# Moving the first stage of batch 2 to later groups, in quarter tiles of the array

## The chip, the cores and the metric

One core of one Trainium2 chip runs the whole program. The metric is device time in microseconds (us) from the start to the end of one launch. The engines are TensorE (PE, its weight loads PEld), VectorE (DVE), ScalarE (ACT), GpSimd (POOL) and SyncE (SP), which issues most of the transfers.

## What is computed

The input x is eight batches of 3008 tokens of 256 float32 values. Each batch is filtered along the tokens by a Fourier transform and then goes through two matrix products with a shrink between them:

```python
X = np.fft.rfft(x, axis=1)
y = np.fft.irfft(X * (filt_r + 1j * filt_i), n=3008, axis=1)
h = y.reshape(24064, 256) @ w_in        # 256 -> 2048
out = (h - np.tanh(h)) @ w_out          # 2048 -> 256
```

## The kernel before

**Stages.** The 3008 tokens are taken as 64 x 47. The transform of a batch has three stages on TensorE. The *first stage* multiplies the 64 direction by constant matrices: r and 47 - r are the upper and lower 64 partitions of one tile, with r from 0 to 23; its result goes to a DRAM tensor `ct1[b]`. The *middle stage* (`middle`, L467 on) reads `ct1`, does the 47 direction, the filter product (four wide multiplications at L489, then L494 to L500) and the way back, and writes `ct2[b]`. The *last stage* (`last`, L565 on; its matmuls at L576) makes the tokens of one group from `ct2`.

**Groups and passes.** A batch has six groups, c = 0 to 5, of up to 512 tokens. The main loop at the end of the kernel goes through 48 groups in passes U of a quarter of the 2048 columns each, so group i has passes 4i to 4i + 3. Pass U computes the first product (`up`, its matmuls at L617 into the banks x, y and z), shrinks the pass before (`shrink`, L739 its multiplications) and computes the second product of the pass before that (`down`, L787). Batch 0's first group uses plain forms (L687 and L842). In a pass, ACT copies x (L623) and VectorE combines: L640 reads bank y, L657 bank z with the third product of x, L665 the last state of x, L673 the last state of z. Banks exist once, so the next pass's product into x waits for L665, and the product that closes z (z<-ut in the trace) waits for L657.

**The order.** It is written out by hand: every engine runs its instructions in program order. A pass has five slots, k = 0 to 4, at which `t(k)` may put one more piece of work. A position is written (c, u, k): group in its batch, pass in the group, slot. First `t` issues up to four transfers of the list `outs` on SP; then it advances one generator: the last stage for the next group at (u, k) = (3, 2), or a step of the first stage when its due position is reached, or a step at a position of `SPLIT_AT`, or the next item of `plan`, the middle stage's list. The plan has fixed kinds of slot: "there" at (2, 0), "back" at (1, 3) and "filter" at (2, 2), (2, 4), (3, 0), (3, 1), (3, 4), (0, 0), (0, 4), (1, 0) and (1, 1). If another piece takes a slot, the plan waits for the next slot of its kind.

**Weights.** They come as 64-bit words and are converted to float32 while the first groups run. VectorE does nearly all of that (L182 to L200, sums at L228 and L231): two instructions at each slot of the first passes and more between, through pass 7.

**First stage, full-array form.** `first` (L277) takes four r at a time: four matmuls of 128 x 128 weights on 256 columns (L297), two into each of the banks t and y; ACT copies both banks (L299) and issues the write of `ct1` itself (L302). Six steps make a batch. Batch 1's last four steps and batch 2's six run from one generator `fs`, due at ten positions between 4 and 31; batch 2's fall into passes 3 (two), 4, 5, 6 and 8. The one of pass 6 lies at the slot (2, 2) of group 1.

**First stage, split form.** `split_first` (L306) takes eight r at a time for batches 3 to 7, on 32 x 32 tiles. It first forms the sum and the difference of two halves on VectorE (L331 and L333, 128 x 1024 each), then runs 32 matmuls (L340) into four banks. ACT copies three banks (L345 to L347), VectorE adds and subtracts (L348, L349), and eight writes go to `outs`. Three steps make a batch; each is five calls of the generator.

A float32 matmul of the program stands as two records of PE in the trace. A timeline row joins records of one group; its start of the next row minus its own start is the time that it holds the engine.

Of the kernel before, what the change touches and what calls it, by code (L numbers as in the profile page):

```python
# [9 lines left out]
F32 = mybir.dt.float32  # L10
# [7 lines left out]
BATCH, SEQ, DM = 8, 3008, 256  # L18
NQ, NR = 64, 47
NA = NQ // 2  # L20
NH = (NR + 1) // 2
# [95 lines left out]
def kernel(  # L117
# [156 lines left out]
        turns[tag] = 1 - turns.get(tag, 1)  # L274
        return kept[tag][:, turns[tag]]

    def first(b, z, also=()):  # L277

        jobs = [*also, *((b, c) for c in range(NX))]

        def begin(k):
            b, c = jobs[k]
            f = tr.tile([128, XH, 128], F32, tag="f", bufs=2, name="f")
            w = XH * 128
            nc.sync.dma_start(f, both_d[:, w * c:w * (c + 1)])
            return load_x(tr.tile([128, XH, DM], F32, tag="x", bufs=2, name="x_sb"),
                          b, XH * c, XH), f

        began = [begin(0), begin(1)]
        yield  # L290
        for k, (b, c) in enumerate(jobs):
            xt, f = began.pop(0)
            banks = z("pf", [128, 2, DM])
            a1 = tr.tile([128, 2, 2, DM], F32, tag="a1", bufs=1, name="a1")
            for m, bank in enumerate(banks):
                for n in range(2):
                    nc.tensor.matmul(bank[:, n], f[:, 2 * m + n], xt[:, 2 * m + n],  # L297
                                     start=True, stop=True)
                ACT.copy(a1[:, m], bank)  # L299
            if k + 2 < len(jobs):  # L300
                began.append(begin(k + 2))
            ACT.dma_start(dram(ct1[b], XH * c * DM, [[NH * DM, 128], [1, XH * DM]]),  # L302
                          a1.rearrange("p m n c -> p (m n c)"))
            yield

    def split_first(b, z):  # L306

        quarters = [slice(32 * k, 32 * k + 32) for k in range(4)]
        for c, tags in enumerate((("t", "o1", "y", "o0"), ("t", "o3", "o1", "o2"),
                                  ("t", "o1", "y", "o0"))):  # L310
            f = tr.tile([128, XH, 128], F32, tag="f", bufs=2, name="f")[:, 0:2]
            f = f.rearrange("p a (b n) -> p (a b) n", n=32)
            nc.sync.dma_start(f, split_d[:, 256 * c:256 * c + 256])
            x0, x1 = (tr.tile([128, XH, DM], F32, tag="x", bufs=2, name="x_sb") for _ in range(2))
            for h, t in enumerate((x0, x1)):
                at = b * SEQ + 32 * h * NR
                for g in range(2):
                    r = 2 * FH * c + FH * g
                    low, high = quarters[g], quarters[2 + g]
                    nc.sync.dma_start(t[low], dram(x.tensor, (at + r) * DM,  # L320
                                                   [[NR * DM, 32], [1, FH * DM]]))
                    lo = int(r == 0)
                    if lo:
                        nc.sync.dma_start(t[high, 0], dram(x.tensor, at * DM,
                                                           [[NR * DM, 32], [1, DM]]))
                    nc.sync.dma_start(t[high, lo:FH], dram(x.tensor, (at + NR - r - lo) * DM,
                                                           [[NR * DM, 32], [-DM, FH - lo], [1, DM]]))
            yield
            both = tr.tile([128, 2, 2, DM], F32, tag="a1", bufs=1, name="a1")
            even = both.rearrange("p v n c -> p (v n) c")  # L330
            V.tensor_add(even, x0, x1)  # L331
            yield
            V.tensor_sub(x1, x0, x1)  # L333
# [12 lines left out]
            ACT.copy(other, banks[1])  # L346
            for g, a1 in enumerate(made):  # L347
                V.tensor_add(a1[:, 0], other if g else banks[0], a1[:, 1])  # L348
                V.tensor_sub(a1[:, 1], other if g else banks[0], a1[:, 1])  # L349
                outs[:0] = [(dram(ct1[b], ((1 - j % 2) * NH + 2 * FH * c + FH * g +  # L350
                                           2 * (j // 2)) * DM,
                                  [[2 * NH * DM, 32], [64 * NH * DM, 2], [1, 2 * DM]]),
                             a1[part].rearrange("p v n c -> p v (n c)"))
                            for j, part in enumerate(quarters)]
                yield

    SPLIT_AT = {(0, 0, 2), (0, 1, 0), (0, 1, 3), (1, 1, 1), (1, 1, 4), (2, 0, 2),
                (3, 0, 2), (4, 2, 0), (4, 2, 2), (4, 3, 0), (5, 0, 2), (5, 1, 0), (5, 1, 3),
                (5, 2, 2)}
# [629 lines left out]
    with tc.tile_pool(name="tr", bufs=2) as tr, tc.manual_schedule():  # L989
# [16 lines left out]
        with tc.tile_pool(name="pro", bufs=1) as pro, \  # L1006
# [230 lines left out]
            rest(0, SG * (last_g - 1), [nc.sync])  # L1237
            way_back()
            rest(SG * (last_g - 1), NA - SG * (last_g - 1), [nc.sync])
            fs = first(2, z2, [(1, c) for c in range(2, NX)])  # L1240
            next(fs)
            convert(100)
            late = weights(tiles1, jobs[5:], G, ahead, 3,
# [6 lines left out]
        with tc.tile_pool(name="dn", bufs=2) as dn, \  # L1250
# [60 lines left out]
                                 start=True, stop=True)  # L1311
            for _ in range(4):
                next(late)
            due = [4 + (LEAD - 4) * k / (NX + 4) for k in range(NX + 4)]
            plan = []
            kinds = {(2, 0): "there", (1, 3): "back"}
            kinds.update({at: "filter" for at in FILTERED})

            firsts, mids = {2: fs}, {}
            for U in range(total + 2):  # L1320
                i, u = divmod(U, 4)
                if U == 6:
# [4 lines left out]
                if U < total:  # L1327
# [5 lines left out]
                    if u == 2 and i + 1 < len(groups) and c + 1 == NC:  # L1333
                        assert not plan
                        e2s[i + 1] = load_e2(*groups[i + 1])
                    if u == 3 and c + 1 == NC and p + 3 < BATCH:
                        firsts[p + 3] = split_first(p + 3, zd4)
                        next(firsts[p + 3])
# [27 lines left out]
                def t(k):  # L1366
# [12 lines left out]
                    if (u, k) == (3, 2) and i + 1 < len(groups):  # L1379
                        next(last(i + 1, z2))  # L1380
                    elif due and due[0] <= pos and (U < 4 or u < 3 and k == 2):
                        due.pop(0)
                        next(firsts[2])
                    elif (c, u, k) in SPLIT_AT and 0 < p < BATCH - 2:
                        next(firsts[p + 2])
                    elif plan and plan[0] == kinds.get((u, k)):
                        plan.pop(0)
                        next(mids[p + 1])
# [58 lines left out]
```

## Time and profile before

| | us |
|---|---|
| median of 3 runs (2563.33 to 2565.52) | 2564.09 |
| the profiled execution, its time | 2566.24 |
| its span, first to last instruction | 2564.4 |
| PE busy | 2540.9 (99%) |
| DVE busy | 1878.4 (73%) |
| ACT busy | 1666.3 (65%) |
| POOL busy | 1481.4 (58%) |

All times below are from the span's start in the profiled execution. The busy share is an average over stages; what a piece of work is worth depends on which engine is full where it stands.

### The profile page before, as it was taken

The numbers are of one execution on the slowest core, as the hardware profiler recorded it, in microseconds if no ns is written. First come the engines' busy times: TensorE is split into PE (matmuls) and PEld (weight loads), VectorE is DVE, ScalarE is ACT, GpSimd is POOL, SyncE is SP. The second block draws the span as 40 slices with busy tenths as digits, with TensorE's granted clock in tenths as the row PEclk, the third lists the DMA queues.
The fourth block names the chain that finished last, engine by engine and source line by source line (L and its number), as shares of the span: only waits on it lengthen the run. The fifth ranks groups of instructions, "written<-read, shape, count | busy, mean of one in ns | idle before, by whom it ended". The sixth has DMA issues, their size and how long they took to land.

```text
span 2564.4 us, 44624 instructions
## 1 busy us (share of the span) xinstructions
PE 2540.9 (99%) x17076; PEld 2177.8 (85%) x17076; DVE 1878.4 (73%) x2265; ACT 1666.3 (65%) x2497; POOL 1481.4 (58%) x1124
## 2 busy tenths in 40 slices
PE   8999999999999999999999999999999999999998
PEld 7678888888898888988888888898889888898887
DVE  6788776887678876788668886688866877555555
ACT  4566666666666666666666666676666666666665
POOL 4256665666466655666656665566645666555552
PEclk9999999999999999999999999999999999999999
DMA  8873214422343323342233322443123322110110
GB/s 221 260 198 103 65 35 109 119 67 48 76 118 93 80 54 94 82 108 67 72 94 90 92 67 61 101 105 97 36 64 88 93 66 52 26 32 18 26 21 19
DMA packets 333660, 212.43 MB, mean 83 GB/s; under 512 B 231737, under 2 KB 304855, under 8 KB 329789
## 3 DMA queue, kind: packets, MB, share of 16 engines
q1 hardware_dynamic: 318511, 184.59, 29.5%
q0 software_dynamic: 11424, 17.03, 2.4%
q10 hardware_dynamic: 3502, 7.87, 0.9%
q8 instruction: 136, 2.23, 0.4%
q14 instruction: 87, 0.71, 0.1%
HBM read 128.75 MB, written 83.39 MB: 83 GB/s over the span
## 4 chain that ended last, share of the span: by engine, by line
PE 94%; DMA 2%; DVE 1%; ACT 1%; issue 1%; POOL 0%; ACTq 0%; POOLq 0%; DVEq 0%
PE o L787 43%; PE x L617 25%; PE z L617 12%; PE y L617 6%; PE pm L401 3%; PE pu L576 2%; DMA ct<-a 1%; PE pm L340 1%; DMA raw<-in_moe_w_in_dram 0%; DMA fh<-f 0%; DMA mats_sb<-mats 0%; PE pe L1089 0%; PE o L842 0%; PE pf L297 0%; PE warm L1038 0%
## 5 line engine op out<-in xcount | busy, mean ns | idle before, releaser
L787 PE MATMUL o<-t,wd 128*128 128x256 f32 (+1 forms) x3008 | 763.6, 377 | 0.0
L597 POOL TENSOR_TENSOR t<-h 128x512 f32<-128x512 f32 (+1 forms) x186 | 305.7, 1643 | 712.4 <-DVE h L739 703.9
L739 DVE TENSOR_TENSOR h<-h,y 128x1024 f32<-128x1024 f32 (+1 forms) x384 | 579.8, 1510 | 160.8 <-ACT y L735 157.3
L787 PEld LDWEIGHTS o<-t,wd 128*128 128x128 f32 x3008 | 569.3, 190 | 85.3 <-POOL o L815 15.1
L617 PE MATMUL x<-tu,wu 128*128 128x256 f32 (+1 forms) x2256 | 576.2, 378 | 0.2 <-ACT u L623 0.2
L787 PE MATMUL o<-h,wd 128*128 128x256 f32 (+1 forms) x2256 | 573.6, 377 | 1.8 <-DVE h L739 1.8
L787 PEld LDWEIGHTS o<-h,wd 128*128 128x128 f32 x2256 | 426.0, 190 | 72.8 <-issue 18.4
L623 ACT COPY s<-x 128x512 f32<-128x512 f32 (+1 forms) x188 | 108.6, 578 | 564.6 <-PE x L617 564.6
L617 PEld LDWEIGHTS x<-tu,wu 128*128 128x128 f32 x2256 | 423.6, 190 | 57.2 <-issue 3.7
L732 ACT ACTIVATE y<-y 128x1024 f32<-128x1024 f32 (+1 forms) x384 | 399.4, 1040 | 12.1
L735 ACT ACTIVATE y<-y 128x1024 f32<-128x1024 f32 (+1 forms) x384 | 399.8, 1041 | 4.6
L729 ACT ACTIVATE y<-h 128x1024 f32<-128x1024 f32 (+1 forms) x384 | 400.5, 1043 | 3.6 <-DVE h L665 1.7
L598 POOL TENSOR_TENSOR t<-h,t 128x512 f32<-128x512 f32 (+1 forms) x186 | 313.9, 1688 | 14.6
L600 POOL TENSOR_TENSOR t<-h,t 128x512 f32<-128x512 f32 (+1 forms) x186 | 303.7, 1633 | 0.0
L599 POOL TENSOR_TENSOR t<-h 128x512 f32<-128x512 f32 (+1 forms) x186 | 289.7, 1557 | 0.0
L623 ACT COPY u<-x 128x512 f32<-128x512 f32 (+1 forms) x376 | 213.3, 567 | 57.0 <-PE x L617 53.7
L665 DVE COPY h<-x 128x512 f32<-128x512 f32 (+1 forms) x188 | 127.8, 680 | 127.2 <-PE x L617 127.1
L617 PE MATMUL z<-tu,wu 128*128 128x256 f32 (+1 forms) x752 | 190.2, 376 | 0.4 <-DVE h L673 0.4
L617 PE MATMUL z<-ut,wu 128*128 128x256 f32 (+1 forms) x752 | 190.2, 376 | 0.4 <-DVE h L657 0.4
L617 PE MATMUL y<-ut,wu 128*128 128x256 f32 (+1 forms) x752 | 190.2, 376 | 0.0
L617 PE MATMUL x<-ut,wu 128*128 128x256 f32 (+1 forms) x752 | 190.2, 376 | 0.0
L657 DVE TENSOR_TENSOR h<-z,u 128x512 f32<-128x512 f32 (+1 forms) x188 | 127.2, 677 | 72.1 <-ACT u L623 71.1
(198 smaller groups left out, 2815.7 us busy)
## 6 DMA issues: line engine op xcount, KB each, us to landing
ft<-filt SPq DMA_DIRECT2D x28, 1024.0 KB
ct<-nn SPq DMA_DIRECT2D x56, 512.0 KB
e<-ct SPq DMA_DIRECT2D x47, 512.0 KB
a<-ct SPq DMA_DIRECT2D x112, 192.0 KB
out_dram<-ot SPq DMA_DIRECT2D x1248, 16.0 KB
x_sb<-in_x_dram SPq DMA_DIRECT2D x110, 128.0 KB
ct<-a SPq DMA_DIRECT2D x60, 128.0 KB
ct<-x_sb SPq DMA_DIRECT2D x60, 128.0 KB
```

What stands on the lines that cost most here:

```text
L597: by.tensor_sub(t[0], b[0][1], b[0][0])
L598: by.tensor_sub(t[1], b[1][1], t[0])
L599: by.tensor_sub(t[2], b[1][1], b[0][1])
L600: by.tensor_sub(t[3], b[1][0], t[1])
L617: nc.tensor.matmul(bank[:, k], wu[:, q - 1, (2 * u + k) * 128:(2 * u + k + 1) * 128], rhs[q - 1], start=(first and k == 0), stop=True, ski ...
L623: ACT.copy(t, X)
L665: V.tensor_copy(h[:, 2, :, 0:w], X)
L729: ACT.activation(y[k], ht[k], AF.Arctan, scale=TURN)
L732: ACT.activation(y[k], y[k], AF.Tanh, scale=BEND)
L735: ACT.activation(y[k], y[k], AF.Square, scale=SCALE, accum_out=y_sums[:, 2 * U + k // 2:2 * U + k // 2 + 1])
L739: V.tensor_mul(ht[k], ht[k], y[k])
L787: nc.tensor.matmul(product(q), wd[:, q - 1, (2 * u + k) * 128: (2 * u + k + 1) * 128], rhs[q - 1][:, k], start=(u == 0 and k == 0 and q == ...
```

## The change

Batch 2's first stage leaves the generator `fs`. `first` now makes steps 2 to 5 of batch 1 alone, at the same four positions as before (4, 7, 10 and 13). A new generator `second_batch` makes batch 2 at the nine positions of `SECOND_AT`, in groups 2 to 5 of batch 0. It has four steps of a new form and one split step:

- `halves_first` takes four r as before, but with weights of 64 x 64: eight matmuls on 256 columns, on the four quarters of the array, the upper and the lower partitions of the data into the two banks t and y. ACT copies bank y, VectorE adds and subtracts (two operations of 128 x 512), and two writes of `ct1` go to the head of `outs`, for SP. Its constants are half as large. It stands at (2, 0, 2), (3, 0, 2), (4, 0, 2) and (5, 0, 2); its first loads are issued at the start of pass 7, the others when a step has run.
- `split_first` with its third step alone, into the banks t, o3, o1 and o2: loads at (5, 0, 3), VectorE's sum and difference at (5, 1, 1) and (5, 1, 2), the matmuls at (5, 2, 0), the rest at (5, 2, 2).

In what follows a step of the new form is called a quarter step. The first one stands where the sixth full-array step stood, in pass 8. The slot (2, 2) of group 1 is no longer taken.

```diff
-    def first(b, z, also=()):
-        jobs = [*also, *((b, c) for c in range(NX))]
+    def first(b, z, at):
+        jobs = [(b, c) for c in at]
...
+    def halves_first(b, z, at):
+        def begin(c):
+            f = tr.tile([128, XH, 128], F32, tag="f", bufs=2, name="f")[:, :, 0:64]
+            nc.sync.dma_start(f, f_d[:, XH * 64 * c:XH * 64 * (c + 1)])
+            return load_x(tr.tile([128, XH, DM], F32, tag="x", bufs=2, name="x_sb"),
+                          b, XH * c, XH), f
+        began = [begin(c) for c in at[:2]]
+        yield
+        for c in at:
+            xt, f = began.pop(0)
+            banks = z("pf", [128, 2, DM])
+            a1 = tr.tile([128, 2, 2, DM], F32, tag="a1", bufs=1, name="a1")
+            for n in range(2):
+                for bank, half in zip(banks, rows):
+                    for m, out_half in enumerate(rows):
+                        nc.tensor.matmul(bank[out_half, n], f[half, 2 * m + n], xt[half, 2 * m + n],
+                                         start=True, stop=True)
+            if c + 2 in at:
+                began.append(begin(c + 2))
+            other = tr.tile([128, 2, DM], F32, tag="e1", bufs=2, name="other")
+            ACT.copy(other, banks[1])
+            V.tensor_add(a1[:, 0], banks[0], other)
+            V.tensor_sub(a1[:, 1], banks[0], other)
+            outs[:0] = [(dram(ct1[b], (XH * c + 2 * m) * DM,
+                              [[NH * DM, 64], [64 * NH * DM, 2], [1, 2 * DM]]),
+                         a1[part].rearrange("p v n c -> p v (n c)"))
+                        for m, part in enumerate(rows)]
+            yield
...
+    def second_batch(z, z4):
+        yield from halves_first(2, z, range(4))
+        yield from split_first(2, z4, ((2, LATE),))
+    SECOND_AT = {(2, 0, 2), (3, 0, 2), (4, 0, 2), (5, 0, 2), (5, 0, 3), (5, 1, 1), (5, 1, 2),
+                 (5, 2, 0), (5, 2, 2)}
...
-            fs = first(2, z2, [(1, c) for c in range(2, NX)])
+            fs = first(1, z2, range(2, NX))
...
-            due = [4 + (LEAD - 4) * k / (NX + 4) for k in range(NX + 4)]
+            due = [4 + (LEAD - 4) * k / (NX + 4) for k in range(4)]
...
+                    if U == 7:
+                        firsts[2] = second_batch(z2, zd4)
+                        next(firsts[2])
...
                     elif due and due[0] <= pos and (U < 4 or u < 3 and k == 2):
                         due.pop(0)
+                        next(fs)
+                    elif (c, u, k) in SECOND_AT and p == 0:
                         next(firsts[2])
```

More of the change, by code (lines that the diff above doesn't have):

```diff
@@ L304, in first, with split_first @@
             yield
-    def split_first(b, z):
+    def halves_first(b, z, at):
[26 more added lines that the diff above has]
+            yield
+    EARLY, LATE = ("t", "o1", "y", "o0"), ("t", "o3", "o1", "o2")
+    def split_first(b, z, steps=((0, EARLY), (1, LATE), (2, EARLY))):
         quarters = [slice(32 * k, 32 * k + 32) for k in range(4)]
-        for c, tags in enumerate((("t", "o1", "y", "o0"), ("t", "o3", "o1", "o2"),
-                                  ("t", "o1", "y", "o0"))):
+        for c, tags in steps:
             f = tr.tile([128, XH, 128], F32, tag="f", bufs=2, name="f")[:, 0:2]
@@ L1317 @@
             kinds.update({at: "filter" for at in FILTERED})
-            firsts, mids = {2: fs}, {}
+            firsts, mids = {}, {}
             for U in range(total + 2):
```

## The prediction

> **What bounds the kernel now.** I read the busy times by stage first, then TensorE's timeline around each step that the change touches, then VectorE's timeline there. In the rows by stage the columns are the window, its length, and the busy time of PE, PEld, DVE, ACT and POOL with instruction counts, then PE's granted clock, the DMA share and GB/s.
>
> ```profile
> core 0: us, PE busy (x) PEld busy (x) DVE busy (x) ACT busy (x) POOL busy (x), PEclk, DMA share, GB/s
> 117.30:155.00 37.70, 37.48 (x189) 24.31 (x189) 36.09 (x71) 24.80 (x42) 25.18 (x28) 1.00 1.01 281
> 155.00:170.50 15.50, 15.50 (x87) 10.49 (x86) 5.66 (x7) 9.69 (x16) 5.68 (x6) 1.00 0.86 244
> 170.50:204.70 34.20, 32.51 (x206) 27.73 (x206) 33.18 (x43) 22.97 (x34) 21.89 (x17) 1.00 0.33 86
> 220.00:429.00 209.00, 209.00 (x1436) 178.11 (x1435) 156.39 (x183) 137.92 (x205) 128.45 (x90) 1.00 0.31 76
> 373.00:380.40 7.40, 7.40 (x70) 5.79 (x69) 5.08 (x7) 5.97 (x11) 4.35 (x4) 1.00 0.00 0
> ```
>
> From 220 us on TensorE has no gap: there, every microsecond of matmul added or taken is one on the total. Before that, two stretches differ. From 117.3 to 155 VectorE is full as well (36.09 of 37.70; the rest is fractions between instructions): it converts weights. From 170.5 to 204.7 it is full again (33.18 of 34.20) and TensorE already waits (32.51). Only from 155 to 170.5 is TensorE alone the limit. So a matmul has three prices, by its place. The change takes six steps out of the early part and puts five into the part where all counts.
>
> ```profile
> 126.36 1.89 PE L297 MATMUL pf<-x_sb,f 128*128 128x256 f32 x8
> 128.09 1.67 PE L842 MATMUL o<-h,wd 128*128 128x448 f32 x4
> ...
> 152.11 1.03 PE L617 MATMUL z<-ut,wu 128*128 128x256 f32 x4
> 152.97 1.10 PE L617 MATMUL x<-ut,wu 128*128 128x256 f32 x4
> ...
> 204.81 1.89 PE L297 MATMUL pf<-x_sb,f 128*128 128x256 f32 x8
> ```
>
> A full-array step occupies TensorE from 126.36 to the next start at 128.09: 1.73 us. Batch 2 has six of them, from the row at 126.36 to that at 204.81: 10.4 us in all. If all of it counted, the change would be a gain.
>
> **Steps one to three** start between 126.36 and the row at 152.11: 5.19 us of TensorE.
>
> ```profile
> 150.47 0.68 DVE L657 TENSOR_TENSOR h<-z,u 128x512 f32<-128x512 f32 x1
> 151.07 1.21 DVE L231 TENSOR_TENSOR wd<-wd 128x256 f32<-128x256 f32 x3
> 152.20 0.68 DVE L665 COPY h<-x 128x512 f32<-128x512 f32 x1
> ```
>
> L665 reads bank x, and the next pass's first product (TensorE's row at 152.97) writes it. VectorE runs its own fixed order without a pause up to here, and none of it is work of the removed steps, so L665 still ends at 152.88. Without the three steps TensorE reaches this point 5.2 us early and waits: the start moves from 152.97 to about 152.9, a gain of **0.07 us**. Where does it wait? Product z at 152.11 needs L657, which ends at 151.15. TensorE would be ready for it at 152.11 - 5.19 = 146.9, a little later if it waits for ACT on the way. That is one idle piece of some 4 us, 0.9 us of work, and 0.8 us more of idleness.
>
> **What the idle piece does to the clock.** In the rows below, earlier in the same run, the clock column falls to 0.50.
>
> ```profile
> 53.00:56.40 3.40, 0.00 (x0) 0.00 (x0) 3.30 (x5) 0.00 (x0) 2.67 (x4) 1.00 0.94 193
> 56.40:59.80 3.40, 2.58 (x6) 2.07 (x7) 3.33 (x4) 0.58 (x1) 2.20 (x3) 0.51 0.98 306
> 59.80:63.30 3.50, 3.50 (x9) 2.61 (x9) 1.72 (x3) 0.59 (x1) 2.21 (x2) 0.50 0.58 188
> 66.70:70.10 3.40, 1.63 (x12) 1.14 (x10) 3.26 (x6) 0.85 (x2) 2.39 (x4) 1.00 0.60 159
> 70.10:73.50 3.40, 2.83 (x7) 2.09 (x7) 3.26 (x7) 0.00 (x0) 0.00 (x0) 0.51 0.83 224
> 73.50:76.90 3.40, 3.40 (x9) 2.55 (x8) 3.23 (x8) 0.58 (x1) 0.00 (x0) 0.50 0.71 246
> ```
>
> A 3.4 us stretch in which TensorE was busy for none, or for 1.63, was followed each time by some 6.8 us at half clock; the first half of each was not quite full (2.58 and 2.83 of 3.40), the second was. The 4 us piece leaves a 3.4 us stretch under half full wherever its bounds fall: the clock should drop between 148.6 (half of 3.4 after 146.9) and 152.2. It comes back after the first full stretch, between 154.0 and 159.0. What lies after 152.9 is on the path at half speed: half of 1.1 to 6.1 us, so 0.5 to 3.0; the middle of where the bounds can fall gives **+1.6 us**. [...]
>
> **Step four:**
>
> ```profile
> 159.50 1.89 PE L297 MATMUL pf<-x_sb,f 128*128 128x256 f32 x8
> ```
>
> It lies where TensorE alone is the limit and VectorE is busy 5.66 of 15.5: **-1.73 us**.
>
> **Step five** lies in the second stretch that VectorE fills; TensorE's row, then VectorE's behind it:
>
> ```profile
> 175.08 1.89 PE L297 MATMUL pf<-x_sb,f 128*128 128x256 f32 x8
> ```
>
> ```profile
> 178.75 0.69 DVE L657 TENSOR_TENSOR h<-z,u 128x512 f32<-128x512 f32 x1 [0.38 <-ACT u L623]
> 179.35 0.75 DVE L231 TENSOR_TENSOR wd<-wd 128x256 f32<-128x256 f32 x2
> 180.46 0.69 DVE L665 COPY h<-x 128x512 f32<-128x512 f32 x1 [0.36 <-PE x L617]
> 181.07 1.22 DVE L739 TENSOR_TENSOR h<-h,y 128x1024 f32<-128x1024 f32 x1
> 182.20 1.22 DVE L489 TENSOR_TENSOR nn<-xy,ft 128x1024 f32<-128x1024 f32 x1
> ```
>
> Its removal gives VectorE back its two waits behind it, 0.38 and 0.36. But the step held a slot, (2, 2) of this group, that is also a filter slot of the middle stage. Freed, it takes the filter product now at 182.20; every later one moves one slot up, and one more (1.22 us) falls into the full stretch ahead of the last wait of TensorE on it. Net **+0.48 us**; bounds: -0.74 if the extra product finds room, +1.22 if the waits stay.
>
> **Step six** (204.81) is replaced in its place by the first quarter step.
>
> **What is added.** The trace has no quarter step of 256 columns, but the last stage's product has the same tiles, 64*64 in two banks, 64 records of 64 columns: as many columns in all as the quarter step's 16 of 256.
>
> ```profile
> 244.90 0.59 PE L787 MATMUL o<-t,wd 128*128 128x256 f32 x2
> 245.43 1.16 PE L576 MATMUL pu<-gt,e 64*64 64x64 f32 x64
> 246.52 1.13 PE L617 MATMUL x<-tu,wu 128*128 128x256 f32 x4
> 247.49 1.24 PE L787 MATMUL o<-t,wd 128*128 128x256 f32 x5
> ```
>
> From 244.90 to 247.49 is 2.59 us; two 256-column records take 0.43 (an eighth of 1.73 each) and four 0.86, so the product costs 1.30 with the pauses where the tiling changes. A split step of batch 3 stands between these two rows:
>
> ```profile
> 427.66 0.92 PE L617 MATMUL x<-tu,wu 128*128 128x224 f32 x4
> ...
> 430.91 0.92 PE L617 MATMUL z<-ut,wu 128*128 128x224 f32 x4
> ```
>
> That is 3.25, less 0.75 for the four records of 224 columns and 0.86 for four of 256 that lie there too: **1.63 us** for a split step. I take **1.30 us** for a quarter step; bounds 0.86 (four records side by side, no pause) and 1.63. Step six's replacement thus gives 1.30 - 1.73 = **-0.43**, three quarter steps in groups 3 to 5 **+3.90**, the split step **+1.63**. They stand in the stretch with 209.00 busy of 209.00, and nothing covers them.
>
> **Other engines.** ACT loses twelve copies and gains seven. A quarter step gives VectorE two operations of 0.69; at its place VectorE waits for ACT's copy anyway, and I cost them at nothing (1.4 us each if that cover were gone). The split step adds two wide ones in pass 21, ahead of the copy at L665 that frees bank x for pass 22:
>
> ```profile
> L333 DVE TENSOR_TENSOR x_sb<-x_sb 128x1024 f32<-128x1024 f32 x15 | 31.6, 2106 | 0.0
> L331 DVE TENSOR_TENSOR a<-x_sb 128x1024 f32<-128x1024 f32 x15 | 23.6, 1573 | 0.0
> ```
>
> ```profile
> 380.43 0.68 DVE L665 COPY h<-x 128x512 f32<-128x512 f32 x1
> ```
>
> ```profile
> 381.90 1.03 PE L617 MATMUL x<-ut,wu 128*128 128x256 f32 x4
> ```
>
> They take 1.57 + 2.11 = 3.68; VectorE idles 7.40 - 5.79 = 1.61 of the time there, and L665 ends 0.79 before its bank is wanted, so TensorE waits 3.68 - 1.61 - 0.79 = 1.28 at most. Other cover may exist: **+1.0**, bounds 0 and 1.3. SP's queue gets fewer loads early (TensorE never waited for them); later each quarter step puts its two writes of ct1, which wait for VectorE's subtraction, at the head of the output list. Behind them wait output stores alone, and nobody reads these before the next group's transposes: no cost. In the split step eleven transfers at most stand behind VectorE's subtraction of the last quarter step; that is a rival.
>
> **The sum**: -0.07 + 1.6 - 1.73 + 0.48 - 0.43 + 3.90 + 1.63 + 1.0 = **+6.4 us**. The profiled execution took 2566.24 (span 2564.4); the median of the runs is 2564.09. Carried onto the median: **2570.5 us**, 0.25% slower. A measurement of this kernel tells about 0.2%, 5.1 us, from no change.
>
> **The rivals.**
>
> *No half clock.* The idle piece breaks up, or the clock holds: +4.8, 2568.9. For it: ACT may split the piece. Against it: both rows with under half a stretch of work were followed by 0.5. Chance 0.20.
>
> *The early steps count after all: faster.* If VectorE has 5 us of room between 117 and 155, TensorE's saving is whole: -10.4 + 4 x 1.30 + 1.63 = -3.6, 2560.5. It decides from the point where VectorE's 36.09 of 37.70 would fall below about 32. Only 1.6 us are idle, scattered. Chance 0.05.
>
> *The split step's loads are late.* They are issued after the last quarter step, and only three slots later VectorE's addition needs them. If they land 2 us late, VectorE stands, and with it L665: 2 us more, 2572.5. Against it: queue SP was idle in this stretch (DMA share 0.00 from 373.0). Chance 0.12.
>
> *The quarters do not run side by side.* Eight products one after the other take twice a full step, 3.46: four times 2.16 more, 2579.1. Against: the 64*64 row above. Chance 0.03.
>
> The forecast itself has 0.60, with 2568.5 to 2572.5 as its own range. Range for 8 in 10: 2567.0 to 2573.3. Slower by over 0.2% (above 2569.2): most of the forecast, the late loads and the serial quarters, and part of the first rival, 0.66. Within 0.2%: 0.29. Faster: 0.05.
>
> **What would show it.** PEclk at 0.5 for some microseconds near 150 to 159, and idle TensorE before it, waiting for VectorE at L657; a DVE timeline up to 155 that has not moved; the first product after it within 0.1 us of 152.9; at step five's place L489 in its stead; quarter steps 1.3 us apart; L665 late around 384. Wrong would be: VectorE's conversions ending earlier than 154, quarter steps well over 1.6 us, or TensorE gaps beyond 1.3 us in groups 2 to 5.

## The result, and the profile after

The changed kernel takes 2570.80 us (median of 9 runs, 2569.72 to 2574.22) against 2564.09 us (9 runs, 2563.33 to 2568.03). The ratio is 1.0024, with a 95% interval of 1.0015 to 1.0032: slower by 6.7 us in the medians and 6.2 by the ratio, where +6.4 was forecast. A second set gave 2571.45 us (7 runs) against 2565.09, ratio 1.0027 (1.0016 to 1.0039). The profiled execution took 2570.06 us, span 2568.3. In the changed kernel the lines named in the prediction from L489 on stand 38 lower down in the file: L617 is now L655, L657 is L695, L665 is L703, L576 is L614. The split step's addition and subtraction (L331, L333) are L363 and L365, and the quarter step's matmuls are at L323. In the experiments the numbers differ from these by a few lines.

The rows by stage of the changed kernel, columns as before:

```profile
113.00:150.80 37.80, 31.83 (x158) 18.61 (x157) 35.99 (x71) 21.47 (x36) 28.42 (x31) 0.97 0.64 170
145.00:148.40 3.40, 0.00 (x0) 0.00 (x0) 3.33 (x9) 0.00 (x0) 0.59 (x1) 1.00 0.74 177
148.50:151.91 3.41, 2.85 (x7) 2.12 (x8) 3.38 (x7) 0.00 (x0) 0.00 (x0) 0.50 1.06 255
151.90:155.30 3.40, 3.40 (x14) 2.43 (x13) 1.12 (x2) 2.75 (x4) 0.00 (x0) 1.00 0.70 211
167.20:200.00 32.80, 29.71 (x191) 24.59 (x190) 32.56 (x44) 20.33 (x30) 20.27 (x16) 1.00 0.55 134
216.00:425.00 209.00, 208.72 (x1489) 174.26 (x1488) 160.26 (x188) 136.36 (x203) 122.66 (x87) 1.00 0.39 96
```

VectorE is as full as before in the first stretch (35.99 of 37.80), and TensorE is no longer full: 31.83 busy, against 37.48. The row from 145.00 is the idle piece, the next one is at half clock. From 216 us on TensorE is full again but for 0.28 us.

TensorE's timeline of the changed kernel at the places that the forecast named:

```profile
142.53 1.67 PE L880 MATMUL o<-h,wd 128*128 128x448 f32 x4
149.06 2.07 PE L655 MATMUL z<-ut,wu 128*128 128x256 f32 x4 [4.86 <-DVE h L695]
150.93 1.53 PE L655 MATMUL x<-ut,wu 128*128 128x256 f32 x4
...
198.22 1.03 PE L655 MATMUL x<-tu,wu 128*128 128x256 f32 x4
...
201.24 0.59 PE L825 MATMUL o<-t,wd 128*128 128x256 f32 x2
201.77 1.09 PE L323 MATMUL pf<-x_sb,f 64*64 64x256 f32 x16
202.79 1.13 PE L655 MATMUL x<-tu,wu 128*128 128x256 f32 x4
...
382.43 1.13 PE L655 MATMUL x<-ut,wu 128*128 128x256 f32 x4 [0.23 <-DVE h L703]
...
2488.05 1.16 PE L614 MATMUL pu<-gt,e 64*64 64x64 f32 x64
```

The kernel before, at two places that the comparison below needs:

```profile
201.36 1.03 PE L617 MATMUL x<-tu,wu 128*128 128x256 f32 x4
...
2485.16 1.16 PE L576 MATMUL pu<-gt,e 64*64 64x64 f32 x64
```

The row at 149.06 holds the wait that the forecast described, 4.86 us for L695, and its four records take twice their time, 2.07 against 1.03. A quarter step runs from about 201.67 (two records after 201.24) to 202.79: 1.12 us, and 0.10 more in the row behind it, 1.13 against 1.03: 1.22 in all.

**How the traces are compared.** I compare by three marks, each the same record in every kernel: the product z<-ut that closes pass 4 (152.11 before, 149.06 after; called Z3), the product x<-tu 3.45 us ahead of step six (201.36 before, 198.22 after; mark 2), and the last product of the last stage (2485.16 before, 2488.05 after). Between mark 2 and the last product the change costs 6.02 us. Up to mark 2 it seems to gain 3.14 us, but the experiments show that this differs by 7 us between executions of kernels that are the same up to there. Here are the marks of all traces, and the part from mark 2 to the last product against before:

| kernel | first full-array step | Z3 | mark 2 | last product | mark 2 to last, against before |
|---|---|---|---|---|---|
| before | 96.90 | 152.11 | 201.36 | 2485.16 | 0 |
| before_again | 93.78 | 150.53 | 200.58 | 2484.42 | +0.03 |
| late_too | 96.34 | 151.62 | 201.77 | 2494.41 | +8.84 |
| free_slots | 94.65 | 150.29 | 200.43 | 2483.76 | -0.47 |
| after | 93.14 | 149.06 | 198.22 | 2488.05 | +6.02 |
| after_again | 92.14 | 146.90 | 197.06 | 2486.87 | +6.00 |
| sub_later | 93.87 | 152.62 | 204.23 | 2494.61 | +6.58 |
| split_gone | 93.07 | 149.46 | 200.20 | 2487.20 | +3.19 |
| early_gone | 94.25 | 151.49 | 200.77 | 2482.88 | -1.70 |
| full_late | 93.15 | 150.80 | 201.62 | 2494.08 | +8.65 |
| six_quarters | 93.00 | 150.77 | 200.56 | 2489.97 | +5.61 |
| split_later | 94.16 | 149.53 | 199.62 | 2488.20 | +4.78 |
| filler | 93.28 | 150.00 | 198.62 | 2488.43 | +6.01 |
| filler_22 | 96.24 | 153.10 | 203.32 | 2493.12 | +6.00 |

VectorE in the changed kernel, at step five's old place and around the split step:

```profile
179.07 1.22 DVE L527 TENSOR_TENSOR nn<-xy,ft 128x1024 f32<-128x1024 f32 x1
...
374.13 1.38 DVE L363 TENSOR_TENSOR a<-x_sb 128x1024 f32<-128x1024 f32 x1 [1.14 <-DMA x_sb<-in_x_dram]
...
377.98 1.21 DVE L365 TENSOR_TENSOR x_sb<-x_sb 128x1024 f32<-128x1024 f32 x1
...
381.69 0.68 DVE L703 COPY h<-x 128x512 f32<-128x512 f32 x1
```

The addition at L363 waits 1.14 us for its x rows, the subtraction stands ahead of the copy L703, and L703 ends at 382.37, just before bank x is taken at 382.43.

### The profile page after: what moved, and what is told of

Read it like the earlier page. It is cut to its first block, busy times and chain, and to the rows that moved or that the text cites. A ratio compares the mean times of both kernels' runs of the same rounds, so it can differ in the third digit from the quotient of the medians.

```text
span 2568.3 us, 44800 instructions
## 1 busy us (share of the span) xinstructions
PE 2536.6 (99%) x17156; PEld 2164.8 (84%) x17156; DVE 1887.3 (73%) x2279; ACT 1663.2 (65%) x2492; POOL 1480.7 (58%) x1124
## 4 chain that ended last, share of the span: by engine, by line
PE 92%; DVE 3%; DMA 2%; POOL 1%; ACT 1%; issue 0%; SPq 0%; ACTq 0%; POOLq 0%; DVEq 0%
PE o L825 43%; PE x L655 25%; PE z L655 12%; PE y L655 6%; PE pm L439 2%; PE pu L614 2%; PE pm L372 1%; DMA filt<-in_filt_r_dram 1%; DMA x<-in_x_dram 0%; POOL filt L1331 0%; DVE h L777 0%; DMA ct<-e 0%; PE o L880 0%; DVE wd L231 0%; DMA ct<-a 0%
## 5 line engine op out<-in xcount | busy, mean ns | idle before, releaser
L655 PE MATMUL x<-tu,wu 128*128 128x256 f32 (+1 forms) x2256 | 576.4, 378 | 0.0
L655 PEld LDWEIGHTS x<-tu,wu 128*128 128x128 f32 x2256 | 422.5, 190 | 59.7 <-issue 5.4
L703 DVE COPY h<-x 128x512 f32<-128x512 f32 (+1 forms) x188 | 127.8, 680 | 125.2 <-PE x L655 125.1
L655 PE MATMUL z<-ut,wu 128*128 128x256 f32 (+1 forms) x752 | 191.3, 377 | 5.9 <-DVE h L695 5.9
L655 PE MATMUL x<-ut,wu 128*128 128x256 f32 (+1 forms) x752 | 190.8, 376 | 1.5 <-DVE ut L622 1.1
L655 PE MATMUL z<-tu,wu 128*128 128x256 f32 (+1 forms) x752 | 190.1, 375 | 1.1 <-DVE h L711 1.1
L655 PE MATMUL y<-ut,wu 128*128 128x256 f32 (+1 forms) x752 | 190.0, 375 | 0.0
L695 DVE TENSOR_TENSOR h<-z,u 128x512 f32<-128x512 f32 (+1 forms) x188 | 127.1, 676 | 59.8 <-ACT u L661 58.9
```

The lines of the kernel that those rows point to most:

```text
L655: nc.tensor.matmul(bank[:, k], wu[:, q - 1, (2 * u + k) * 128:(2 * u + k + 1) * 128], rhs[q - 1], start=(first and k == 0), stop=True, ski ...
L703: V.tensor_copy(h[:, 2, :, 0:w], X)
```

## The experiments

The theory is the forecast's: what is taken from the early part was mostly hidden, what is added late costs TensorE's own time plus some stalls in pass 21. The main rival was that the two parts differ in another way: that the early steps were worth much more, or that the late ones cost loads and evictions and not TensorE time.

**early_gone**: the early part alone.

```diff
-            fs = first(2, z2, [(1, c) for c in range(2, NX)])
+            fs = first(1, z2, range(2, NX))
-                              dram(ct1[b], (PLACE[q] * NA + 8 * o) * NH * DM,
+                              dram(ct1[b if b != 2 else 1], (PLACE[q] * NA + 8 * o) * NH * DM,
```

> The kernel before with the six full-array steps of batch 2 left out of groups 0 and 1 and nothing put in their place: batch 2's middle stage reads batch 1's first-stage rows, so batch 2's own first stage is left out of the computation. Theory (as the prediction has it: steps one to three lay beside VectorE's chain, step four and step six cost 1.73 us of TensorE each, step five gives back 0.74 us but frees filter slot (2,2) for 1.22 us, and the idle piece at position 22 brings a stretch of half clock for 0.5 to 1.6 us): from the first full-array step to the last product of the last stage 1.5 to 3.0 us shorter than before, the time 2561 to 2563 us. If VectorE's chain to Z3 of pass 4 is itself longer without the steps (it looked about 1.6 us longer in the trace of the changed kernel), 0.5 to 1.5 us shorter. Rival one (all the TensorE time of the six steps counts): 10.4 us shorter, 2554 us. Rival two (VectorE has 5 us of room): 6 to 7 us shorter.

Measured: 2563.88 us (10 runs) against 2565.09; ratio 0.9994 (0.9984 to 1.0003). 10.4 us of TensorE work are gone, and the time falls by 1.5 us by the ratio, at most 4.1; it stays above the 2561 to 2563 us that the theory gave. The forecast's terms for this part make -0.07 + 1.6 - 1.73 + 0.48 - 1.73 = -1.45. TensorE's timeline:

```profile
151.49 2.07 PE L617 MATMUL z<-ut,wu 128*128 128x256 f32 x4 [5.53 <-DVE h L657]
...
200.77 1.03 PE L617 MATMUL x<-tu,wu 128*128 128x256 f32 x4
...
2482.88 1.16 PE L576 MATMUL pu<-gt,e 64*64 64x64 f32 x64
```

Mark 2 comes 0.59 us earlier than before, the last product 2.28 us: step six alone (1.73) makes most of it. Both rivals fall. My yardstick, the first full-array step, was a bad one: counted from there this kernel is 0.37 us longer than before, because that step came 2.65 us earlier and nothing behind it came as much earlier. VectorE sets the pace there.

**before_again**: the kernel before, unchanged.

> The kernel before once more. In the traces so far the first full-array step starts at 92.1 to 94.3 us where batch 2's steps are not in groups 0 and 1, and at 96.3 to 96.9 us in the two kernels that have them there. Theory (the start of the body follows from where TensorE's stretches of half clock fall in the prologue, which differs from one execution to the next whatever the kernel): the start lies anywhere in 92 to 97 us and the body, from that start to the last product of the last stage, is within 1 us of 2389.2 us. Rival (batch 2's early steps themselves make the start later by some 3 us): the start lies at 96 to 97 us again.

Measured: ratio 0.9999 (0.9990 to 1.0009).

```profile
93.78 1.46 PE L297 MATMUL pf<-x_sb,f 128*128 128x256 f32 x6
...
200.58 1.03 PE L617 MATMUL x<-tu,wu 128*128 128x256 f32 x4
```

The first step starts 3.12 us earlier than in the first trace of the same program, so the rival falls: the start is not set by batch 2's steps. But the body is 2.38 us longer, outside the 1 us that I gave, and mark 2 differs by only 0.78. Hence the marks on the absolute scale.

**after_again**: the changed kernel, unchanged.

> The changed kernel once more, for how far the prologue, the clock's stretches and the body differ from one execution to the next. Theory: the body within 0.5 us of the first trace's (6.6 us longer than before), the first full-array step anywhere within 4 us, since the clock's stretches in the prologue come at other times. Rival: the half-clock stretch near 150 us is not there in this execution, and the body is 0.5 us shorter.

Measured: the second set of the first section. The first step starts at 92.14, the body is 6.47 us longer than before, and the part from mark 2 on costs +6.00, against +6.02. The half clock was there too and lasted twice as long, 144.96 to 151.78. The theory holds, the rival falls.

**late_too**: the late part alone, on top of the kernel before.

```diff
+    SECOND_AT = {(2, 1, 2), (3, 0, 2), (4, 0, 2), (5, 0, 2), (5, 0, 3), (5, 1, 1), (5, 1, 2),
+                 (5, 2, 0), (5, 2, 2)}
...
+                    if U == 9:
+                        firsts[2] = second_batch(z2, zd4)
+                        next(firsts[2])
...
-                        next(firsts[2])
+                        next(fs)
+                    elif (c, u, k) in SECOND_AT and p == 0:
+                        next(firsts[2])
```

> The kernel before with the changed kernel's four quarter steps and its split step in addition, the first quarter step at position (2,1,2); batch 2's first-stage rows are written twice. Theory (where TensorE is the bound, an added step costs its own TensorE time): 4 x 1.22 + 1.63 + 0.3 to 0.7 for the loads and the subtraction of the split step = 6.8 to 7.2 us longer over the body, about 2571 us. Rival (the late steps are partly hidden beside other work, and the early part of the change costs more than thought): 3 to 5 us longer.

Measured: 2578.14 us (4 runs), ratio 1.0047 (1.0030 to 1.0064). In the trace +8.84 us from mark 2 on, more than either theory said. Three quarter steps cost 1.22 each, the split step and its stalls 2.47, as in the changed kernel, and 0.38 follow near 740 us. The first quarter step, at (2,1,2), cost 2.30:

```profile
219.13 0.66 PE L323 MATMUL pf<-x_sb,f 64*64 64x256 f32 x6
220.22 1.07 PE L323 MATMUL pf<-x_sb,f 64*64 64x256 f32 x10 [0.44 <-DMA x_sb<-in_x_dram]
221.22 1.13 PE L655 MATMUL x<-tu,wu 128*128 128x256 f32 x4
```

Its eight products stop after three for x rows that have not landed. This kernel starts the loads with pass 9 and not with pass 7, so they are issued from 214.61 on, 4.5 us ahead of the step: the 1.08 us beyond the other quarter steps' 1.22 go with that wait. So the late part is not hidden anywhere, and a step whose load is issued too late costs that too. The 13 us of the medians are not all explained: the profiled execution is 11.4 us longer than before's, 9.25 of it at the last product and 2.2 behind it, where TensorE's rows are the same in both. With four runs I leave the rest open.

**full_late**: six full-array steps in place of the quarter steps and the split step.

```diff
-        yield from halves_first(2, z, range(4))
-        yield from split_first(2, z4, ((2, LATE),))
+        yield from first(2, z, range(NX))
...
+    SECOND_AT = {(2, 0, 2), (3, 0, 2), (4, 0, 2), (5, 0, 2), (5, 1, 2), (5, 2, 2)}
```

> The changed kernel with six full-array steps, as the kernel before has them, in place of the four quarter steps and the split step: at (2,0,2), (3,0,2), (4,0,2), (5,0,2), (5,1,2) and (5,2,2). Theory (TensorE never waits from 206 us on, so a step there costs its own TensorE time, whatever its form): 6 x 1.73 = 10.4 us of body instead of the changed kernel's 1.12 + 3 x 1.22 + 2.46 = 7.2 us for the same work, so 3.1 us longer than the changed kernel, about 2574 us; each step a rise of 1.73 us. Rival (what costs is not TensorE's time but the loads, evictions and writes of a step, which are alike in both forms): within 1 us of the changed kernel.

Measured: 2575.17 us (5 runs), ratio 1.0037 (1.0024 to 1.0051). From mark 2 on +8.65, five steps of 1.73 (the first equals step six); 2.63 more than the changed kernel (I had left its 0.38 us near 740 us out of the 3.1). One of them:

```profile
258.97 1.89 PE L298 MATMUL pf<-x_sb,f 128*128 128x256 f32 x8
260.70 1.03 PE L654 MATMUL x<-tu,wu 128*128 128x256 f32 x4
```

The quarter form is the cheaper one; it is the place that costs. The rival (alike in both forms) falls.

**six_quarters**: two more quarter steps for the split step.

```diff
-        yield from halves_first(2, z, range(4))
-        yield from split_first(2, z4, ((2, LATE),))
+        yield from halves_first(2, z, range(NX))
...
+    SECOND_AT = {(2, 0, 2), (3, 0, 2), (4, 0, 2), (5, 0, 2), (5, 1, 2), (5, 2, 2)}
```

> The changed kernel with two more quarter steps, at (5,1,2) and (5,2,2), in place of the split step. Theory (a quarter step costs 1.22 us and brings no stall, the split step 1.62 us and 0.84 us of stalls around it, and the 0.38 us near 740 us go with the split step, since they were not there without it): the same as the changed kernel at 400 us, 0.4 us shorter over the body. Rival (any first-stage step in pass 21 or 22 makes L665 late there): 0.5 to 0.8 us longer than the changed kernel.

Measured: 2571.30 us (10 runs), ratio 1.0023 (1.0014 to 1.0033). From mark 2 on +5.61, 0.41 less than the changed kernel, as the theory had it. There is no wait in pass 21, and the last step costs what the first did:

```profile
391.96 0.59 PE L823 MATMUL o<-t,wd 128*128 128x256 f32 x2
392.49 1.10 PE L323 MATMUL pf<-x_sb,f 64*64 64x256 f32 x16
393.51 1.13 PE L653 MATMUL x<-tu,wu 128*128 128x256 f32 x4
```

**split_gone**: the split step left out.

```diff
-        yield from split_first(2, z4, ((2, LATE),))
...
+    SECOND_AT = {(2, 0, 2), (3, 0, 2), (4, 0, 2), (5, 0, 2)}
...
-                              dram(ct1[b], (PLACE[q] * NA + 8 * o) * NH * DM,
+                              dram(ct1[b if b != 2 else 1], (PLACE[q] * NA + 8 * o) * NH * DM,
```

> The changed kernel without its split step: batch 2's middle stage reads batch 1's first-stage rows, so two of the six parts of batch 2's first stage are not computed and the other four not used. Theory (the split step costs its own TensorE time and the stalls near it, and the 0.38 us that the changed kernel loses near 740 us has another cause): 2.4 to 2.6 us shorter than the changed kernel at 400 us, 2.2 to 2.6 us over the body. Rival (the 0.38 us belong to it): 2.8 to 3.0 us over the body.

Measured: 2568.92 us (10 runs), ratio 1.0014 (1.0004 to 1.0023). At 400 us it is 2.46 us shorter than the changed kernel from mark 2 on, over the whole 2.83 (the table's +3.19 against +6.02).

The rival is right: the 0.38 us near 740 us come with the split step, though they fall 360 us later, in a split step of another batch.

**sub_later**: the subtraction two slots later.

```diff
-    SECOND_AT = {(2, 0, 2), (3, 0, 2), (4, 0, 2), (5, 0, 2), (5, 0, 3), (5, 1, 1), (5, 1, 2),
+    SECOND_AT = {(2, 0, 2), (3, 0, 2), (4, 0, 2), (5, 0, 2), (5, 0, 3), (5, 1, 1), (5, 1, 4),
```

> The changed kernel with the split step's subtraction at (5,1,4) instead of (5,1,2). Theory (the prediction's last term: the subtraction and the late addition ahead of L665 make bank x of pass 22 late): the stalls of 0.61 us in pass 21 and pass 22 shrink to 0.1 to 0.3 us, the body is 0.3 to 0.5 us shorter than the changed kernel's. Rival (what is late is the split step's x rows, through the addition): the stalls stay, body within 0.1 us.

Measured: 2574.09 us (6 runs), ratio 1.0033 (1.0021 to 1.0045). The 0.40 us of stalls ahead of pass 22 went, as the theory said, but from mark 2 on it is 0.56 us longer, not shorter. TensorE shows the new wait:

```profile
388.91 1.03 PE L655 MATMUL y<-ut,wu 128*128 128x256 f32 x4
389.86 0.61 PE L372 MATMUL pm<-a,f 32*32 32x256 f32 x2
390.94 0.40 PE L372 MATMUL pm<-x_sb,f 32*32 32x256 f32 x1 [0.47 <-DVE x_sb L365]
```

The split step's second matmul needs the difference, and VectorE has not finished it. Neither theory had that. Another 6.0 us of its trace lie ahead of mark 2 (204.23 against 198.22), where the two programs are the same. Its median lies 2.6 to 3.3 us above those of the changed kernel; the wait makes 0.56 of that, and the rest is open.

**split_later**: addition, subtraction and matmuls all later.

```diff
-    SECOND_AT = {(2, 0, 2), (3, 0, 2), (4, 0, 2), (5, 0, 2), (5, 0, 3), (5, 1, 1), (5, 1, 2),
-                 (5, 2, 0), (5, 2, 2)}
+    SECOND_AT = {(2, 0, 2), (3, 0, 2), (4, 0, 2), (5, 0, 2), (5, 0, 3), (5, 1, 2), (5, 1, 4),
+                 (5, 2, 1), (5, 2, 2)}
```

> The changed kernel with the split step's addition at (5,1,2), its subtraction at (5,1,4) and its matmuls at (5,2,1). With the subtraction alone at (5,1,4) the 0.40 us of stalls ahead of the matmuls were gone, but the matmuls waited 0.5 us for the subtraction. Theory (the addition no longer waits for its x rows, the subtraction no longer stands ahead of L665, and the matmuls come one place later): 0.3 to 0.5 us shorter than the changed kernel at 400 us. Rival (the matmuls wait for the subtraction here too): as long as the changed kernel or 0.1 to 0.6 us longer.

Measured: 2570.60 us (10 runs), ratio 1.0020 (1.0011 to 1.0030). VectorE first, then TensorE:

```profile
378.12 1.23 DVE L363 TENSOR_TENSOR a<-x_sb 128x1024 f32<-128x1024 f32 x1
381.85 0.68 DVE L703 COPY h<-x 128x512 f32<-128x512 f32 x1
...
383.91 2.25 DVE L365 TENSOR_TENSOR x_sb<-x_sb 128x1024 f32<-128x1024 f32 x1
```

```profile
386.77 1.03 PE L655 MATMUL x<-tu,wu 128*128 128x256 f32 x4
...
389.15 1.13 PE L655 MATMUL z<-tu,wu 128*128 128x256 f32 x4
```

The addition waits for nothing, the subtraction stands behind L703. Between the two products lie 2.38 us, less 0.86 for the first; with 0.10 in the row behind, the split step costs 1.62 and no stall. From mark 2 on it is 1.24 us shorter than the changed kernel: 0.84 of stalls and the 0.38 near 740 us, which go here although the split step is there. So, as far as one kernel shows, they hang on when it stands, not that it is there; in the changed kernel a subtraction of batch 4's split step waits 0.47 us there, and why is not settled. Nor is it settled how the 0.84 divide between the late x rows and the subtraction, since both moved.

**filler**: TensorE work at the three freed positions.

```diff
+                    elif pos in (16, 19, 22) and i < 2:
+                        fill = zd("fill", [128, 2, DM])
+                        for n in range(4):
+                            nc.tensor.matmul(fill[:, n % 2], wu[:, 0, 0:128], wu[:, 0, 0:256],
+                                             start=True, stop=True)
```

> The changed kernel with four 128 x 128 x 256 matmuls, never read, at each of the freed positions 16, 19 and 22 (as much TensorE work as a full-array step, with no load, no VectorE and no ScalarE work behind it). Theory (the freed position 22 leaves TensorE idle long enough for a stretch of half clock, and that is what the changed kernel pays there): the granted clock stays at 1.00 from 113 to 170 us, and the body is 0.5 to 1.6 us shorter than the changed kernel's, about 2569.5 us. Rival (VectorE's chain to Z3 of pass 4 is longer because its work is spread otherwise, and the clock matters little): clock 1.00 but body within 0.3 us of the changed kernel's. Rival two: TensorE has no room there after all, 1.7 us per position longer, up to 5 us.

A window of the stage and the timeline:

```profile
149.40:152.80 3.40, 2.21 (x9) 1.65 (x10) 3.37 (x7) 0.00 (x0) 0.00 (x0) 1.00 0.99 225
```

```profile
150.00 1.13 PE L655 MATMUL z<-ut,wu 128*128 128x256 f32 x4 [1.86 <-DVE h L695]
151.72 1.13 PE L655 MATMUL x<-ut,wu 128*128 128x256 f32 x4 [0.60 <-DVE h L703]
```

The clock stays at 1.00, and TensorE still waits 1.86 us for VectorE: 5.2 us of matmuls cost nothing there, so rival two falls. Measured: 2572.16 us (9 runs), ratio 1.0023 (1.0012 to 1.0033): no shorter than the changed kernel, and 0.24 us longer in the body, as the first rival said, though that is the doubtful yardstick. The clock's part follows below.

**filler_22**: eight matmuls at position 22 alone.

```diff
+                    elif pos == 22 and i < 2:
+                        fill = zd("fill", [128, 2, DM])
+                        for n in range(8):
```

> The changed kernel with eight matmuls of 128 x 128 x 256, never read, at position 22 alone (3.46 us of TensorE work in the 5 us that it waits there). Theory (TensorE waits for VectorE there, so the filler costs nothing, and it keeps the clock at 1.00; the five traces without batch 2's steps lost 0.5 to 3.0 us, 1.6 us in the mean, to half clock between Z3 of pass 4 and 157 us): clock 1.00 from 113 to 200 us, 1 to 2 us shorter than the changed kernel in the mean, about 2569.5 us. Rival (the time before Z3 of pass 4 differs so much from run to run that the clock's part cannot be told in the times, or something else takes it): ratio to before within 0.0005 of the changed kernel's.

Measured: 2572.11 us (11 runs), ratio 1.0024 (1.0015 to 1.0033). The experiment missed: the clock fell all the same. The filler ended at 146.67, and a stretch with 1.42 us of work in 3.42 came behind it; so the times decide nothing between theory and rival.

```profile
151.28:154.70 3.42, 1.42 (x5) 0.68 (x4) 3.35 (x10) 0.00 (x0) 0.00 (x0) 1.00 0.94 187
154.70:158.11 3.41, 3.28 (x8) 2.66 (x9) 1.67 (x3) 1.17 (x2) 0.00 (x0) 0.50 1.08 220
```

**free_slots**: batch 2's steps put where they should cost least.

```diff
-            due = [4 + (LEAD - 4) * k / (NX + 4) for k in range(NX + 4)]
+            due = [4, 7, 10, 13, 16, 19, 22, 32, 33]
...
+    SECOND_AT = {(2, 0, 2)}
```

> The kernel before with batch 2's steps put elsewhere: three full-array steps at positions 16, 19 and 22 as before, the fourth at (1,2,2) and the fifth at (1,2,3), the sixth as a quarter step at (2,0,2); the step at position 25 and the last full-array step are gone. Theory (a full-array step beside VectorE's chain is free, the one that lay at position 25 cost 1.73 us, the last 1.73 against 1.22 us): 1.0 to 2.2 us shorter than before, 2562.5 to 2564 us. Rival (the fifth step's eviction waits until the fourth's rows have landed, since both use the one buffer a1, and TensorE waits for the bank): 1 to 3 us longer than before.

Measured: 2565.43 us (11 runs), ratio 1.0000 (0.9991 to 1.0009): no gain. The fourth and the fifth step:

```profile
172.43 1.89 PE L296 MATMUL pf<-x_sb,f 128*128 128x256 f32 x8
174.16 1.03 PE L652 MATMUL x<-tu,wu 128*128 128x256 f32 x4
175.02 1.89 PE L822 MATMUL o<-t,wd 128*128 128x256 f32 x8
176.75 1.89 PE L296 MATMUL pf<-x_sb,f 128*128 128x256 f32 x8
```

Step four's 1.73 us are won, but here 1.72 are lost again: of two steps in the second stretch that VectorE fills, only one is free. TensorE does not wait between them, so the rival (the one buffer a1) falls; 0.47 come back with the quarter step. None of the versions that do the whole work beats the kernel before; early_gone, which leaves batch 2's first stage out, gains only 1.5 us, at most 4.1.

## Why the prediction was right, point by point

**Steps one to three** (-0.07). That VectorE hides them is shown by early_gone and by the filler. The number itself is open. Z3 stands at 150.08 in the mean of the eight kernels without early steps and fillers, and at 151.42 in the three with all six: 1.3 us, with 5.7 us between the first and the last of the eight (146.90 and 152.62). The forecast took VectorE's own time as given, and that is not quite so. The last 101 operations of VectorE up to the one that Z3 waits for (L657, now L695) are the same in all kernels; VectorE was busy with them for 52.2 to 53.2 us in the four traces with steps there, and for 52.7 to 55.4 in the eight (53.9 in filler, whose first rival had spoken of this). Why they last longer is not settled.

**Half clock** (+1.6, bounds 0.5 to 3.0). All eight show it, none of the four with work there (before, before_again, late_too, free_slots). The next mark is the product z<-tu of pass 5, first before, then in the changed kernel:

```profile
157.13 1.03 PE L617 MATMUL z<-tu,wu 128*128 128x256 f32 x4
155.52 1.03 PE L655 MATMUL z<-tu,wu 128*128 128x256 f32 x4
```

From Z3 to there it is 5.82 to 5.93 us at clock 1.00 (before_again, late_too, free_slots, filler; 5.02 in before, where Z3 came 0.96 us behind L657's end and not at once), and 6.46 to 8.91 in the eight, 7.51 in the mean: +1.6 over 5.9, from 0.5 to 3.0. The size was right as a mean; the changed kernel's own trace shows 0.5. The way it comes about was right too: in seven of the eight the loss is half of the half clock that is left behind Z3, less the 0.9 us that TensorE waits there anyway (in filler it starts x at 151.72, 1.72 behind Z3, for a product of 0.86). In the changed kernel 2.85 us are left, from 149.06 to 151.91, and the loss is 0.54; in split_gone 6.04, from 149.46 to 155.50, and the loss is 2.12. In the eighth, sub_later, the half clock starts behind Z3. The duration was not right: I had 6.8 us of half clock, and two of the eight traces, the changed kernel's among them, show one stretch of 3.4. "No half clock" falls as a rival. The times of filler are no shorter all the same: the start differs from run to run by more than the 1.6 us that one would have to read there.

**Step four** (-1.73): 1.73 less at its place in all eight.

**Step five** (+0.48): the filter product took the slot, as the row at 179.07 shows; the cost from step five to the end of that stretch is +0.21 in all eight. The term was 0.27 too large; which part of it, no run shows.

**Step six** (-0.43) **and three quarter steps** (+3.90): a quarter step costs 1.22, not 1.30, so -0.51 and +3.66. The 64*64 row was the right one to read; the products run side by side (sixteen records in 1.22 us, where eight of a full-array step take 1.73), and that rival falls.

**Split step** (+1.63): 1.62.

**The stall in pass 21** (+1.0, bounds 0 to 1.3): 0.84 around the split step and 0.38 near 740 us, 1.22 in all. L703 was late, as said, but that wait, with the slower row behind it, makes 0.50 only; three pauses of 0.11 and the 0.38 were not foreseen, so that the whole comes this near to 1.0 is luck. The rival "loads late" was in part true as well: the x rows came 1.14 us after VectorE was ready, though SP's queue had been idle (no issue from 353.84 to 365.20; the eight loads were issued from 367.19 to 371.41); I had given that 0.12 and 2 us of its own, and split_later shows that it cannot cost more than the 0.84.

**The sum.** From mark 2 on the terms make -0.43 + 3.90 + 1.63 + 1.0 = 6.10; measured 6.02. Two errors cancel there: the quarter steps cost 0.32 less and the stalls 0.22 more. Up to mark 2 the terms make -0.07 + 1.6 - 1.73 + 0.48 = +0.28; the eight traces reach it at 200.29 in the mean (197.06 to 204.23), the three with all steps at 201.24 (200.58 to 201.77): -0.95, not told from +0.28 by so few traces. Together with the 6.02, -0.95 makes 5.1 and +0.28 makes 6.3; the medians differ by 6.7 and 6.4. They agree with the forecast's +6.4 better than they can be expected to: the changed kernel, filler and filler_22, alike from mark 2 on to 0.02 us, have medians from 2570.80 to 2572.16, and from the last product to the end of the span it is 79.2 us in before, 80.3 in the changed kernel and up to 81.5 elsewhere, with the same rows of TensorE. That the sum fits to 0.3 us is luck; that it lies near 6 is not.

**The signs.** Of the signs that the forecast named, half clock after a wait for L657, L489 at step five's place, the quarter steps' distance and a late L665 (382.4) came. Two did not: the first product behind the idle piece starts at 150.93, not near 152.9, and VectorE's copy at L665 moved from 152.20 to 150.05. That is not the change alone: in before_again, the same program as before, that copy starts at 151.41. The sign against it, conversions that end earlier than 154, could tell nothing in this stretch, for in the kernel before they end at 152.28 (the row at 151.07, 1.21 long).

## What to carry to other kernels

Price a matmul by what limits its place: here the same step was free beside a full VectorE and cost its whole 1.73 us a pass later, so a cheaper form (1.22) moved to a dearer place lost. When comparing two traces, take marks that the same program reaches at the same time in two executions; a start that varies by 4 us, or one that nothing depends on, makes a false zero. And when a step is moved or put off, look at all its inputs: the load issued just ahead of (2,1,2) and the subtraction at (5,1,4) each made a wait where there had been none.

## What the runs showed of the hardware that was not expected

**When the half clock ends.** Near 150 us it lasted one stretch of 3.41 us in the changed kernel and in early_gone, and two in the other six of the eight. Two windows at half clock, of early_gone and of full_late, and the one behind the latter:

```profile
151.15:154.56 3.41, 3.07 (x7) 2.33 (x8) 3.38 (x7) 0.00 (x0) 0.00 (x0) 0.50 1.03 214
```

```profile
150.19:153.60 3.41, 2.80 (x7) 2.07 (x8) 3.38 (x7) 0.00 (x0) 0.00 (x0) 0.50 1.09 233
153.60:157.02 3.42, 3.42 (x9) 2.47 (x8) 1.07 (x2) 2.35 (x3) 0.00 (x0) 0.50 0.47 167
```

With 3.07 of 3.41 the clock came back, with 2.80 it did not. In between the busy time does not tell: with 2.85 it came back in the changed kernel (the row at 148.50), and in sub_later (153.58 to 157.00, 2.85 of 3.42) it did not. In the other direction 1.42 of 3.42 brought half clock (filler_22), while 2.25 of 3.41 did not (filler, 149.43 to 152.84); here 1.65 brought it in before (66.72 to 70.14) and 1.64 did not in early_gone (144.32 to 147.73). At which amount of work the clock changes, these rows show only roughly. One stretch cost 0.5 and 0.7 us behind Z3, two cost 1.2 to 3.0.

**VectorE beside GpSimd.** One operation takes 0.43 us, or in some cases 0.54 to 1.17. Two rows of VectorE in the changed kernel, and what GpSimd does then:

```profile
110.01 0.43 DVE L185 TENSOR_SCALAR xy<-xy 128x512 int32<-128x512 int32 x1
...
115.83 1.07 DVE L185 TENSOR_SCALAR xy<-xy 128x512 int32<-128x512 int32 x1
```

```profile
115.36 1.30 POOL L1331 DMA_DIRECT2D filt<-in_filt_i_dram  x1
116.65 0.60 POOL L1327 DMA_DIRECT2D filt<-in_filt_r_dram  x1
```

Every slow case that I looked at (L182, L185 and L191 from 110 to 200 us in before, after, early_gone and full_late, 15 of 71) lies wholly inside such GpSimd work, but so does about half of the 56 quick ones. Before has one of them, the other three kernels four to six; VectorE sets the pace up to Z3, so they may be one source of the spread there. No run tested it. None shows what makes the slow cases slow.
